# Convolving four channel blocks of the first token group on TensorE by diagonal tap matrices, with the first scores in two pieces and a new order table

## The chip, the cores and the metric

The kernel runs on one core of one Trainium2 chip. The metric is the time of one execution on the device in microseconds (us), the median over runs. The core has a matrix engine (TensorE, PE in the views; its weight loads are shown apart as PEld), a vector engine (VectorE, DVE), an activation engine (ScalarE, ACT), GpSimd (POOL) and a queue that issues DMAs (SyncE, SP). Each engine works through its own list of instructions in order; semaphores make one engine wait for another.

## What is computed

Attention with a local window and a few global keys, then a feed-forward block with a convolution along the tokens, then a gated block that mixes along the tokens. Cut to what matters here:

```
attn = softmax(scale * q @ k.T - slope * dist, on kept keys) @ v     # (2, 8, 768, 64)
x    = attn, heads joined                                            # (2, 768, 512)
h    = relu(x @ w_in)                                                # 1024 channels
conv = sum over j of conv_w[j] * h shifted by j - 1 along the tokens # 3 taps, per channel
y    = (h * sigmoid(conv)) @ w_out
u, v = halves of relu(y @ w2_in); v normalised over channels
out  = (u * (w_spatial @ v + b)) @ w2_out
```

Here `conv` is the part that moves to another engine.

## The kernel before

The tokens go in six groups of 256 (two batches of three). Group g passes through these stages.

- Attention (`tick`, `scores`, `soften`, `turn_p`, `weigh`, `turn_x`). A unit u is a pair of heads of one group, a step s one of its two tiles of 128 queries. `scores` (L789) makes the scores of both steps in float32; `soften` adds the bias and takes the lowest (L808 on VectorE), then the exponential (L826 on ScalarE); `turn_p` transposes them on TensorE (L839), `weigh` multiplies by v (L894 for the first two groups, in float32), and `turn_x` transposes the result (L942).
- First product (`inner`, L1017): 12 matmuls in float16 (parts high and low) make one block of 128 channels; there are 8 blocks in a group. Then, for that block, a relu moves it out of PSUM into the tile `hp` (L1361). The convolution follows: `middle` (L1024, on ScalarE or VectorE) writes the middle tap back into the PSUM bank, `sides` (L1030, two VectorE instructions) adds the outer two. Tanh (L1050), the gate (L1055) and the split into two float16 parts follow.
- Second product (`outer`, L1087), then the last block (`normal` L1171, `columns_u` L1382, `seventh` L1294, `last` L1444) for the whole batch.

The order of the instructions on each engine is not left to a scheduler. Python code lists the tasks with planned costs, and the table `ORDER`, a string found by a search beforehand, says which task comes next and on which engine it runs, and which PSUM bank it uses. Everything is emitted in this order, so each engine's queue is fixed by the table. Where the plan leaves TensorE idle within its first 70 us, `Plan.emit` puts in matmuls whose result nobody reads (`warm`, L988, the tile `hl`). They are called fillers below. Their count follows from the planned costs, not from what happens on the chip.

At the start, VectorE builds the masks from two counts that a small DMA brings: `word` (L567), then on TensorE `spread` (L570) copies them to all partitions, then `words` (L573) and `masks` (L578 to L585), then two biases (L594). The instructions of `flags` (L635, L637, L625) only check the counts for a branch at the end.

Of the kernel before, what the change touches and what calls it, by code (L numbers as in the profile page):

```python
# [17 lines left out]
ALU = mybir.AluOpType  # L18
# [29 lines left out]
BIASES = 2  # L48

# [58 lines left out]
def sub_cost(n):  # L108
# [6 lines left out]
    "CHSAAGAWSDnGAnSAXGABDACGAZSADDAuSAbGAgSAEDBHGCMDAFPAGDCJA0CIGAHDAaP12AJDAKAASAAIDAMAAoGAdDBaSApA3AyDAYSANGAcDAOA",  # L115
    "A2P45AzDA3SAeACKDALGAfACLDAqDA1AAwP6CNSATGAQABIDBhP12BMSBJDA0ABdDARGA-SBLABeDBKAArDEHGBFP0APGBgABbP4BfABGDAhGAxA",
    "CUP53CQDAUAAsDBcAB0DAVGBwP0AiA6BzDD9SCRDB3P4CpGDgSBxAAjDAtGCTAAkDCSAByGB1AA4GCrDCnP2A5A1BiSB4DCuP0BpSAlAA6DBTSCo",
    "AAmGCqDB2AA7DCtACOP6BOA4CvDBNGB5SDhP21CsAA_GDBDCPADADA8AC-P0BPDDDACVP3DYP6ECDC_ABQDDCADxDCWACZSBRADwDDWP5DzADZDD",
    "EP0DXAEBDDaP4DFADeP5BqGBAA1DGDCXDEEABjGBBDDbABkA6A9GDcDEFP20EDAAvSDfDDyABSGBCDBVA3DiP4FJSBlDDjAD_P1B7A5B6GDkDEAA",
    "BUGERDEPP4BmDBDADmP1EQAB8DCwSBnACASBWDEGP6DoAB9DDpABXDB-AD0P4EhDEIACgSB_GBYAESDDISDqDEJAEeSElP53ETABEGEUAEKDD2AE",  # L120
    "-P2DrAD1GEiDELADsDD3AEMDEWGCYABoGE6DBrA0E7DEfP1D4DEkAEVP6CxGEjABZGEgAFYDFXDD5AE4P3BsDEXACyA1DJGEvP5D6DEYABtDCBGE",
    "5ACzDC3SFaAEmP4E_DCCA0DtAEZDE8AFbP32DuGE9AEwGC0DFZAEnGCaGEoACDDEaAFVP1D7AC1DEpAFtDFWAC4GFsDExAF5DFqP1HbGEyAEbDCh",
    "GF6DBuAFAP6C2GCEDFrAEzDCbA3DPSFBGF9P20BvGF2SF7AEqDFvAFCAFwP1ENACcDFuAEOGE0AGIDErAGJDFDACdDGKGEcAD8GCFAFxDF3P3EdG",
    "CeAE1DCGGF4AEsDFEDCiA1GcP54E2ACfGC5A3GXDGYDHYSGMACjDFhP0FKGE3GF8AG3SC6DDKA2JzSGZGFcGGTSCkDFFADQGGLAKuSFGDEtAGGP1",
    "ClDGVAGNP6C7DGHAGWGGsDGbAGtDDRA1DLDCmGGxP3GaAG6DFjAG7DHZADSDEuGC8ADMDGuGFdP5GwAD-SF-P4C9GDTDGvAFyP2FzPDNAGODF0PF",
    "iGG4AF1PDOGGyDGCPF_AGzP1FkAG0PGADFHAG5GG_P63FlDFeAGpADHAFfDG8GGdP4GqGIQSHmDG1PGeAHnDHAP5FmAGDPGfDG9AG2PFIGGrSHOD",
# [1596 lines left out]
```

## Time and profile before

| what | value |
|---|---|
| median of 3 runs | 346.46 us (346.24 to 347.46) |
| profiled execution, its own time | 346.18 us |
| its span in the profile | 344.4 us |
| TensorE busy | 336.9 us, 98% of the span, 2824 matmul records |
| VectorE busy | 305.3 us, 89% |
| ScalarE busy | 244.0 us, 71% |
| GpSimd busy | 140.6 us, 41% |

The span runs from the first to the last instruction of the program; the execution's own time holds some 1.8 us more around it. Busy times are shares of the whole span, an average over stages with different limits. Matmul records overlap, because matmuls are pipelined: the mean duration of a record is not the time that it adds to the stream, and a busy TensorE may be working at fillers.

### The profile page before, as it was taken

To read this page: it belongs to the slowest core of one execution; us is meant where nothing else is said; L and a number is where in the kernel's file an instruction comes from. 1 tells how busy PE (TensorE), PEld (TensorE's weight loads), DVE (VectorE), ACT (ScalarE), POOL (GpSimd) and SP (SyncE) were. 2 spreads that over 40 slices of the span, in tenths; PEclk is the share of its full clock that TensorE was granted. 3 is DMA by queue.
4 is the path that set the end of the run, shared out by engine and by line. 5 is a ranking of instruction groups with operands and counts; after the bars stand their busy time and mean duration, and the time that the engine had idled before them with its cause. 6 is when DMAs were issued, how large, how long until landed. Compare 5 with 4: busy or idle time off the path is not lost.

```text
span 344.4 us, 7937 instructions
## 1 busy us (share of the span) xinstructions
PE 336.9 (98%) x2824; PEld 246.5 (72%) x2824; DVE 305.3 (89%) x892; ACT 244.0 (71%) x619; POOL 140.6 (41%) x233
## 2 busy tenths in 40 slices
PE   8999999999999999999999999999999999999993
PEld 5888779898888888888996757755556666654451
DVE  6999999999999999999988899999998999999400
ACT  4999999999999999999865552776555233334331
POOL 5747698599757877737451000000124012010000
PEclk9999999999999999999999999999999999999998
DMA  7999638799659984645770000001461000000332
GB/s 246 349 386 300 214 105 302 175 209 256 125 149 205 278 173 79 184 79 109 102 221 0 2 1 0 2 1 48 126 206 52 0 2 0 3 30 0 124 124 101
DMA packets 46115, 43.62 MB, mean 127 GB/s; under 512 B 34674, under 2 KB 36466, under 8 KB 45554
## 3 DMA queue, kind: packets, MB, share of 16 engines
q1 hardware_dynamic: 46064, 43.02, 45.7%
q8 instruction: 24, 0.39, 0.5%
q14 instruction: 25, 0.20, 0.2%
q10 hardware_dynamic: 2, 0.00, 0.0%
HBM read 31.48 MB, written 3.15 MB: 101 GB/s over the span
## 4 chain that ended last, share of the span: by engine, by line
PE 96%; DMA 1%; DVE 0%; ACT 0%; issue 0%; DVEq 0%
PE bank L1017 19%; PE bank L1087 18%; PE bank L1294 12%; PE bank L1444 9%; PE bank L1382 9%; PE bank L1171 9%; PE bank L789 7%; PE bank L894 4%; PE bank L839 2%; PE bank L988 2%; PE bank L942 2%; DMA qk_dt_float<-in_qk 1%; PE bank L900 1%; PE bank L901 1%; PE bank L902 1%; ACT wk_dt_float L454 0%
## 5 line engine op out<-in xcount | busy, mean ns | idle before, releaser
L1017 PE MATMUL bank<-x_dt_float,w1h_dt_float 128*128 128x260 f16 (+1 forms) x384 | 65.5, 273 | 0.0
L1087 PE MATMUL bank<-hh_dt_float,w2h_dt_float 128*128 128x256 f16 (+2 forms) x192 | 52.4, 273 | 0.0
L1017 PE MATMUL bank<-x_dt_float,w1l_dt_float 128*128 128x260 f16 (+1 forms) x192 | 52.4, 273 | 0.0
L1087 PE MATMUL bank<-hl_dt_float,w2h_dt_float 128*128 128x256 f16 (+2 forms) x192 | 52.3, 272 | 0.0
L1087 PE MATMUL bank<-hh_dt_float,w2l_dt_float 128*128 128x256 f16 (+2 forms) x192 | 52.3, 272 | 0.0
L1030 DVE SCALAR_TENSOR_TENSOR bank<-hp_dt_float,cwt,bank 128x254 f32<-128x254 f32 (+2 forms) x96 | 46.1, 486 | 3.3 <-ACT bank L1024 0.6
L470 POOL TENSOR_TENSOR ph_dt_float<-sb_dt_float,ph_dt_float 128x512 f16<-128x512 f32 x29 | 34.2, 1184 | 20.5 <-ACT ph_dt_float L456 12.4
L1017 PEld LDWEIGHTS <-w1h_dt_float 128*128 128x128 f16 x384 | 37.1, 97 | 5.7
L1087 PEld LDWEIGHTS <-w2h_dt_float 128*128 128x128 f16 x384 | 36.3, 98 | 5.4 <-issue 0.3
L808 DVE CUSTOM_DVE_ANT_0 sb_dt_float<-bank,bias_dt_float 128x256 f32<-128x256 f32 (+1 forms) x96 | 35.4, 402 | 1.6 <-PE bank L789 1.3
L1382 PE MATMUL bank<-ys_dt_float,w3uh_dt_float 128*128 128x384 f16 x128 | 31.2, 326 | 0.0
L826 ACT ACTIVATE sb_dt_float<-sb_dt_float,nb_dt_float 128x256 f32<-128x256 f32 (+1 forms) x64 | 29.6, 491 | 0.0
L659 POOL TENSOR_SCALAR raw_dt_float<-raw_dt_float 128x512 int32<-128x512 uint8 x28 | 19.0, 680 | 24.7 <-DMA raw_dt_float<-in_w 22.0
L1444 PE MATMUL bank<-w4h_dt_float,g_dt_float 128*128 128x512 f16 (+1 forms) x104 | 28.8, 363 | 0.0
L1171 PE MATMUL bank<-w3vh_dt_float,ys_dt_float 128*128 128x512 f16 x96 | 28.5, 379 | 0.0
L470 POOL TENSOR_TENSOR hl_dt_float<-ac_dt_float,hh_dt_float 128x254 f16<-128x254 f32 (+2 forms) x35 | 23.4, 678 | 10.7 <-DVE hh_dt_float L460 8.0
L1444 PEld LDWEIGHTS <-g_dt_float 128*128 128x128 f16 x156 | 15.2, 98 | 15.4
L1171 PEld LDWEIGHTS <-ys_dt_float 128*128 128x128 f16 x144 | 14.1, 98 | 15.3
L1294 PE MATMUL bank<-ws_dt_float,vn_dt_float 128*128 128x384 f16 x144 | 25.0, 326 | 0.0
L1050 ACT ACTIVATE bank<-bank 128x254 f32<-128x254 f32 (+2 forms) x48 | 16.9, 364 | 10.5 <-DVE bank L1030 10.2
L1024 ACT ACTIVATE bank<-hp_dt_float,cwt 128x254 f32<-128x254 f32 (+2 forms) x44 | 21.0, 477 | 0.5
L1055 DVE SCALAR_TENSOR_TENSOR ac_dt_float<-bank,hp_dt_float 128x254 f32<-128x254 f32 (+2 forms) x48 | 19.5, 418 | 2.0 <-ACT bank L1050 1.5
(198 smaller groups left out, 907.6 us busy)
## 6 DMA issues: line engine op xcount, KB each, us to landing
raw_dt_float<-in_w SPq DMA_DIRECT2D x20, 512.0 KB, 6.3
qk_dt_float<-in_qk SPq DMA_DIRECT2D x24, 336.0 KB, 4.6
v_dt_float<-in_vb SPq DMA_DIRECT2D x4, 1024.0 KB, 5.7
out_x<-wk_dt_float SPq DMA_DIRECT2D x11, 256.0 KB, 2.0
raw_dt_float<-in_wst SPq DMA_DIRECT2D x6, 384.0 KB, 3.8
raw_dt_float<-in_w3v SPq DMA_DIRECT2D x4, 512.0 KB, 5.5
raw_dt_float<-in_w3u SPq DMA_DIRECT2D x4, 512.0 KB, 4.4
v_dt_float<-in_vb SPq DMA_DIRECT2D x2, 768.0 KB, 5.1
```

The source lines that it names most:

```text
L470: self.engines[e].tensor_tensor(out=out, in0=in0, in1=in1, op=ALU.subtract)
L789: nc.tensor.matmul(self.ps(sp[h])[:, 256 * t : 256 * (t + 1)], x[r, t * P : (t + 1) * P], y[r, k0[t] : k0[t] + 256], start=n == 0, stop=n ...
L808: nc.vector.tensor_tensor_reduce(out=sb[:, h, :n], in0=self.ps(self.sp[u][h])[:, 256 * t : 256 * t + n], in1=self.m("bias", 2 * p + h)[:, ...
L826: nc.scalar.activation(out=sb[:, h, :n], in_=sb[:, h, :n], func=AF.Exp, scale=-1.0, bias=nb[:, h : h + 1])
L1017: nc.tensor.matmul(self.ps(acc)[:, :nx], w[f][:, k * P : (k + 1) * P], x[:, k, x0:], start=k == n == 0, stop=k == 3 and n == 2,)
L1024: nc.scalar.activation(out=ac(), in_=near(1), func=AF.Copy, scale=tap(1))
L1030: nc.vector.scalar_tensor_tensor(out=ac(), in0=near(j), scalar=tap(j), in1=ac(), op0=ALU.mult, op1=ALU.add)
L1087: nc.tensor.matmul(ps(), w[2 * d + k // 4][:, k % 4 * P : (k % 4 + 1) * P], x, start=k == n == 0, stop=k == 7 and n == 2,)
L1171: nc.tensor.matmul(ps(), x[:, y, k, tk], w[k], start=n == 0, stop=n == 11)
L1294: self.nc.tensor.matmul(self.ps(acc)[:, :HS], v[:, k, x, ek], w[:, k, y], start=n == 0, stop=n == 8)
L1382: nc.tensor.matmul(ps(), w[e4][:, k * P : (k + 1) * P], x[:, y, k, s], start=n == 0, stop=n == 11)
L1444: nc.tensor.matmul(ps(), x[:, y, k, tk], w[k][:, at], start=n == 0, stop=n == 11)
```

## The change

In group 0, blocks 0 to 3 are convolved on TensorE. For each, GpSimd makes three 128x128 matrices in float32 that hold one tap of each channel on the diagonal (`spread`, 12 instructions in all), and TensorE multiplies them with the three shifted views of `hp` and adds up in the PSUM bank (`convolve`, 12 matmuls of 254 columns in float32). `middle` and `sides` fall away for these four blocks: 4 instructions on ScalarE, 8 on VectorE. The scores of units 0 and 1 become two tasks each, one for each step, with the same matmuls, so that the first step's scores are released sooner. `flags` may not start before a planned 60 us, and the small load of the taps not before 3 us; the planned landing of the first DMA moves from 3.2 to 2.6 us and the planned start of `word` from 3.1 to 2.62 us. `ORDER` was searched anew, so the order of the whole program moves. Of all TensorE instructions only two kinds change in number: 12 tap matmuls come, and the fillers go from 60 to 18. Of these 18, 12 stand ahead of the first scores, 3 and 1 ahead of the first product, and 2 behind the third set of tap matmuls. The last output blocks also change places: before, the last product is 128x512; now it is one of 128x256.

```diff
-    BEGIN, FIRST, TURN = 0.75, 3.2, 2.0
+    BEGIN, FIRST, TURN = 0.75, 2.6, 2.0
...
+            over["ys1"] = ("taps",)
...
-        add(dict(DVE=0.17), word, writes=[("word", 0)], begin=3.1)
+        add(dict(DVE=0.17), word, writes=[("word", 0)], begin=2.62)
...
-            [("craw", 0)], 24576,
+            [("craw", 0)], 24576, begin=3.0,
...
-        add(dict(DVE=1.0), flags, reads=[("word", 0)], writes=[("flag", 0)], both=True)
+        add(dict(DVE=1.0), flags, reads=[("word", 0)], writes=[("flag", 0)], both=True, begin=60.0)
...
-        self.plan.add(dict(PE=cost), products, reads=reads, writes=sp, half=True)
+        if u >= SINGLE:
+            self.plan.add(dict(PE=cost), lambda e: products(range(2)), reads=reads, writes=sp, half=True)
+            return
+        for t in range(2):
+            self.plan.add(
+                dict(PE=0.5 * (cost + 0.283)), lambda e, t=t: products([t]), reads=reads,
+                writes=[(*x, t) for x in sp], half=True,
+            )
...
-        add(dict(ACT=scaled(nout), DVE=dve(nout) + 0.1), middle, reads=[("hp", n), ("cwt", 0)], writes=[acc])
-        add(dict(DVE=0.94), sides, reads=[("hp", n), ("cwt", 0)], writes=[acc])
+        if self.half and g == 0 and f < TAPPED:
+            taps = self.m("taps", f).rearrange("p (j n) -> p j n", j=3)
+
+            def spread(e):
+                for j in range(3):
+                    nc.gpsimd.tensor_scalar(
+                        out=taps[:, j], in0=self.ident, scalar1=tap(j), scalar2=None, op0=ALU.mult
+                    )
+
+            def convolve(e):
+                for j in range(3):
+                    nc.tensor.matmul(ac(), taps[:, j], near(j), start=j == 0, stop=j == 2)
+
+            add(dict(POOL=0.85), spread, reads=[("cwt", 0), ("ident", 0)], writes=[("taps", f)])
+            add(
+                dict(PE=3 * (0.01 + 4 * nout / 2400)), convolve, reads=[("hp", n), ("taps", f)], writes=[acc],
+            )
+        else:
+            add(
+                dict(ACT=scaled(nout), DVE=dve(nout) + 0.1), middle, reads=[("hp", n), ("cwt", 0)], writes=[acc],
+            )
+            add(dict(DVE=0.94), sides, reads=[("hp", n), ("cwt", 0)], writes=[acc])
```

`SINGLE` is 2 and `TAPPED` is 4. The order table moves instructions in three places that matter below.

VectorE at the start of the program, before (`cnt` and `within` are of `flags`, `wf` holds the spread counts, `bias` the first two bias tables):

```order
L561 TENSOR_SCALAR keep_dt_float_80<-rel_dt_float_79 128x288
L562 TENSOR_TENSOR keep_dt_float_80<-keep_dt_float_80,rel_dt_float_79 128x288
L567 CAST word<-wt 1x8
L635 CAST cnt<-wt 1x2
L637 SCALAR_TENSOR_TENSOR cnt<-cnt,word 1x2 x3
L625 TENSOR_SCALAR within<-cnt 1x1 x3
L573 COPY wf<-bank 128x8
L578 TENSOR_SCALAR few<-keep_dt_float_80,wf 128x32
```

The same place now:

```order
L573 CAST word<-wt 1x8
L567 TENSOR_SCALAR keep_dt_float_80<-rel_dt_float_79 128x288
L568 TENSOR_TENSOR keep_dt_float_80<-keep_dt_float_80,rel_dt_float_79 128x288
L579 COPY wf<-bank 128x8
L584 TENSOR_SCALAR few<-keep_dt_float_80,wf 128x32
```

`word` stands ahead of the two 128x288 instructions, and the seven instructions of `flags` are gone from here (they stand some 180 rows further on).

SyncE's first loads, before (`qk` holds queries and keys of a unit, `craw` the taps, `raw` a block of weights, `v` the values):

```order
L514 DMA craw<-in_cw 128x24
L514 DMA qk_dt_float_88<-in_qk 128x672
L514 DMA raw_dt_float_128<-in_w 128x512
L514 DMA qk_dt_float_122<-in_qk 128x672
L514 DMA qk_dt_float_130<-in_qk 128x672
L514 DMA raw_dt_float_126<-in_w 128x512
```

And now:

```order
L520 DMA qk_dt_float_88<-in_qk 128x672
L520 DMA qk_dt_float_122<-in_qk 128x672
L520 DMA qk_dt_float_130<-in_qk 128x672
L520 DMA craw<-in_cw 128x24
L520 DMA raw_dt_float_128<-in_w 128x512
L520 DMA v_dt_float_89<-in_vb 128x12x128
```

The first unit's load is issued first, and the first three units' loads stand ahead of the taps and of all weights.

TensorE behind the first blocks of the first product, before (the last weight load and matmul of a block, then attention work, then the next block):

```order
L1017 LDWEIGHTS w1l_dt_float_99
L1017 MATMUL bank<-x_dt_float_155,w1l_dt_float_99 128x256
L789 MATMUL bank<-qk_dt_float_88 128x256 x4
L894 MATMUL bank<-v_dt_float_89,pt_dt_float_131 128x65 x8
L839 MATMUL bank<-ident,sb_dt_float_132 128x128 x4
```

Now, behind the first block:

```order
L1030 LDWEIGHTS w1l_dt_float_100
L1030 MATMUL bank<-x_dt_float_155,w1l_dt_float_100 128x256
L852 MATMUL bank<-ident,sb_dt_float_123 128x128 x4
L907 MATMUL bank<-v_dt_float_89,pt_dt_float_131 128x65 x8
L1071 MATMUL bank<-hp_dt_float_188,taps_dt_float_189 128x254 x3
L852 MATMUL bank<-ident,sb_dt_float_132 128x128 x4
L795 MATMUL bank<-qk_dt_float_130 128x256 x4
L852 MATMUL bank<-ident,sb_dt_float_139 128x128 x4
L907 MATMUL bank<-v_dt_float_89,pt_dt_float_144 128x65 x8
```

Three tap matmuls stand behind a transpose and a `weigh`, with the relu of their block to be done meanwhile. Two blocks of the first product follow, then six tap matmuls at once; two more blocks later the last three stand directly behind the fifth block's matmuls.

## Rows read from the trace of the kernel before

**Rows 1.** The page: busy us, share of the span and instructions of each engine.

```profile
PE 336.9 (98%) x2824; PEld 246.5 (72%) x2824; DVE 305.3 (89%) x892; ACT 244.0 (71%) x619; POOL 140.6 (41%) x233
```

**Rows 2.** Stretches: length; PE, PEld, DVE, ACT, POOL busy (instructions); clock; DMA.

```profile
40.00:50.00 10.00, 9.87 (x81) 7.61 (x79) 9.82 (x31) 9.97 (x27) 8.23 (x16) 1.00 0.45 135
50.00:60.00 10.00, 9.90 (x87) 8.83 (x87) 9.69 (x31) 10.00 (x24) 8.73 (x16) 1.00 0.74 249
```

**Rows 3.** The same for the fillers (L988) alone: PE and PEld busy (records).

```profile
0.00:8.45 8.45, 4.54 (x23) 2.68 (x23) 1.00 0.71 249
8.45:70.00 61.55, 5.90 (x38) 3.47 (x37) 1.00 0.78 261
```

**Rows 4.** Chain that ended last: start us, length us, what (records).

```profile
1.19 2.10 PE bank L988 x9
...
4.07 1.44 PE bank L988 x6
5.50 2.01 PE bank L789 x8
...
8.49 1.06 PE bank L789 x8
...
13.88 1.73 PE bank L894 x16
15.61 0.44 PE bank L839 x4
...
28.19 3.94 PE bank L1017 x36
...
42.16 0.87 PE bank L988 x8
```

**Rows 5.** Timeline of the start: start us, length us, engine, line, out<-in, count [idle before <-releaser].

```profile
2.61 0.15 DVE L567 CAST word<-wt 1x8 f32<-1x8 uint16 x1
...
3.22 0.59 PE L570 MATMUL bank<-word,ones 1*128 1x8 f32 x2
...
3.85 0.17 DVE L573 COPY wf<-bank 128x8 f32<-128x8 f32 x1 [0.17 <-PE bank L570]
...
5.41 1.11 ACT L603 ACTIVATE bias_dt_float<-rel_dt_float 128x288 f32<-128x288 f32 x3 [2.48 <-DVE rel_dt_float L585]
5.42 0.83 DVE L594 SCALAR_TENSOR_TENSOR bias_dt_float<-rel_dt_float,keep_dt_float 128x288 f32<-128x288 f32 x2
...
7.56 0.33 DVE L808 CUSTOM_DVE_ANT_0 sb_dt_float<-bank,bias_dt_float 128x160 f32<-128x160 f32 x1 [1.31 <-PE bank L789]
...
9.49 0.66 PE L839 MATMUL bank<-ident,sb_dt_float 128*128 128x128 f32 x4
```

**Rows 6.** Loads of `qk` in the first 14 us: issue to landing.

```profile
DMA to landing us min/median/max: 3.2/4.9/7.6
```

**Rows 7.** Groups by line and shape, 20 to 70 us: busy us, mean ns | idle.

```profile
L826 ACT ACTIVATE sb_dt_float<-sb_dt_float,nm_dt_float 128x256 f32<-128x256 f32 x18 | 8.4, 502 | 0.0
L655 ACT ACTIVATE bank<-raw_dt_float 128x512 f32<-128x512 f32 x12 | 7.6, 637 | 0.0
...
L1024 ACT ACTIVATE bank<-hp_dt_float,cwt 128x254 f32<-128x254 f32 x8 | 3.8, 471 | 0.1
...
L1030 DVE SCALAR_TENSOR_TENSOR bank<-hp_dt_float,cwt,bank 128x254 f32<-128x254 f32 x16 | 7.6, 483 | 0.3
```

**Rows 8.** Timeline of TensorE around its two longest waits, columns as in group 5.

```profile
22.40 0.38 PE L988 MATMUL bank<-hl_dt_float 128*128 128x256 f16 x2
22.91 0.44 PE L942 MATMUL bank<-ident,xk_dt_float 128*128 128x128 f32 x2
...
48.94 0.93 PE L988 MATMUL bank<-hl_dt_float 128*128 128x256 f16 x7
50.10 1.14 PE L789 MATMUL bank<-qk_dt_float 64*128 64x256 f32 x8 [0.23 <-DMA qk_dt_float<-in_qk]
```

**Rows 9.** The end: timeline of ScalarE's last copies out of PSUM.

```profile
333.62 0.38 ACT L454 ACTIVATE wk_dt_float<-bank 128x256 f32<-128x256 f32 x1 [2.27 <-PE bank L1444]
...
338.75 0.60 ACT L454 ACTIVATE wk_dt_float<-bank 128x512 f32<-128x512 f32 x1 [1.67 <-PE bank L1444]
```

More of the change, by code (lines that the diff above doesn't have):

```diff
@@ L48 @@
 BIASES = 2
+SINGLE = 2
+TAPPED = 4
 HALF = dict(w=8, x=9, h=12, y=12, g=12, v=8, s=16)
@@ new lines @@
+    "AfAA4PA0DAgABASANGBKDASAAxP4CPSCLA0A2AARGBjP56AhSBLDA1ABfDBMABgDATGBNAAyDBHP2AqA1CKGDpGBdP3ApGCMDB1DBIAB2DB0GCND",
+    "BiAArDAVGB5P4BeAAsDELGB4ABhACSDBrSB3AA6GCTDByP2A7A0DiSB6DCQP3BOSCVACWP15A8DBVSBBGCUACRAD3GD5GA9DBzACpP4CtDBCA6B7",
+    "SCXP3CrGCsDDjP02DDDCuADCDAiGCvABDDCqADAP1DEADzDCwP4DyDDFABEDAjA5EDDD1ACCSEEDBFAD_SDYP6AkDDBAEHP02CxDBPGDZAEGABsG",
+    "AlDDaP1CYAD0AETDBWGBkSEFAEUDEgSCZDAtAFLSAmDEWADGP6B8GDbDEBP4BXA5DgP3AnGEjDDHABQA1BYDECAFMGEkDCDGBRDEmAERP0AwSA-A",
+    "EnP24DhDEVADIDBlGElABSDEhP3ESAAuGDkP6E9DEiADcP1CbSFaDE6P0DlAE8DFdP34A_GDdADmDCaADeDE7AFZDEaGE_AEIP1BZDGVSE-AF4SF",
@@ new lines @@
+    "vDBmA6FuDCiSFXP2BTDFxABnDFAP5BUGEKAFwAF7DFbABoDB9A0BaDCySFcAEMPF8DBbGBpAFBDFYAB-DFsP6DrGF-AF_P45BtA3B_DCcGDJABuD",
+    "DKSENABGGF5P2FtAGKDFyP0EODF9AGaDBqGDfAGZDEPABvDCAAEQGDoP6GLDCdA4C5SF6DEyGCzGCkA3CeDC0A5CBGD2P1FzDDqABwACfDDLGDsP",
+    "CEA2C1DGMGD4ACjGCgACFDBxGD6PDtAC2DDMA0DuDGbGGOAClDC6GGeP45GNACGDChGD7AGcACmDGIP6GXAHaSGPP2DNDDRSDvAGYGCnAD8DGJAG",
+    "vDGuDDwGGdAFfP3G8DCHAGzP6EYGG9DFeGFgAGwGGQDEpGCIGC7A1FhDC3AC8DGAP4G-GGyAEASC4GGfP5DODEXP2GxAG6AC9DG_AG0DG7GHBP30",
+    "HAAGrAEZDHMDGBAEoP1ISSHbAHpDGsGHoDG5SGgAGCDD9AGhDEbPHcGGtSEqAHPDErAHQDDnAEsDHCP6EcAFCP4D-GFRAEdDHRGHDAFSDEtAExP5",
@@ new lines @@
+    "HTAFDGFEDHNGEeAEuDFFAHEDFNAFGDIKP3FkGEfGHOSEzAFTAFODEvAFjP0E0AFUDHSAE1DEwGFHAFPAF0P2DSGF1PDTA1FIDF2PFQDFlAF3PE2A",
+    "HtP64HmACODDxAFmAGEPE3DHnGJLSITADUDICP5GWSFJAH8DHqGILACoGIYDHsAFnDGGP4E4AGHPHrAE5GGRPDVDFoAGSPC-AIUGGTPFpDGFPDPA",
+    "H7DHUP1IDDIMAIXDFqAIAP0FKDH4AH9GINDFrGGUPH-AGjPDWAIZGIgP6IBDH5GIEAIaAHVDIbAH6SIzGGnPDQGIOAIFDGkPIhAIcP01GlAH_AIP",
+    "DDXGIiDIGAGoPIVAHWP7I1DI0DHXPIwAIjDIWGIdP3HYPHiAHZPJMAIHDHyPI2GIxDHzPIIAH0PIkAJSDJNGH1PIySIeAGmDHvP5HgAI7P1IlDJR",
+    "DH2AI3AIfDI4AJTDHjDJWP26JPAHhDKESJUAG1P0I8AH3DJQGJVAG2PJvDJuDG3PFVAI9DI5P3JwGKKDC_GKJDIoP7IQAI6DGpAJqAKLGHuGI-DJ",
@@ L170 @@
+    "P4cfDcYDdSDdKP7clDcoDc4DdjP6b5DczDdXDdsP2a3Dc0DcsDamDdkDdlDdvP5dTDdtAc5DbiAduScFDanDbjAcGGavDctP6dwAa8Da9DbkAb_D",
+    "dmDb6Ac1P3dnDcBAcrDcuDcHAdpP2c-DcNAdLDcTAdMDcaAcADc_DcgAdEP5dADdqAcZDcmAdrSdBDdxSddP4dCDc6Dc8Ac7DdFDd4P6c2DdeDdY",
+    "DdZDd1P7dfDdUDdaDdbDdGDdHDdyP1dgDd2AdNDdODdIDdhDd9P2dzAd5AdDAd6SdJAdPAeDP3dVAdcAd-AdiAd_SeAP0d0SdoAd3Sd7P4eGP5d8",
+    "DeBAeCSeMP7eHAeEAeFSeJP1eNAeOSePP6eKAeLSeISeQAeRS",
 )
@@ L366, in __init__ @@
         m.place(0, ("g0", 3072, 1), ("g1", 3072, 1))
+        m.place(m.at["ys1"][0], ("taps", 3 * P, 8))
         end = m.place(uv, ("u0", 3072, 1), ("vn0", 3072, 1))
@@ L509, in decide, with load @@
         self.plan.add(dict(DVE=6.0), judge, reads=[acc, ("flag", 0)], writes=[("junk", 0)])
-    def load(self, out, in_, writes, size, reads=()):
+    def load(self, out, in_, writes, size, reads=(), begin=0.0):
         self.plan.add(
             dict(SP=Plan.ISSUE), lambda e: self.nc.sync.dma_start(out=out, in_=in_), reads=reads, writes=writes,
-            load=0.05 + size / Plan.RATE,
+            load=0.05 + size / Plan.RATE, begin=begin,
         )
@@ L782, in scores, with products @@
         sp = self.sp[u] = [self.plan.next("ps") for _ in range(2)]
-        def products(e):
-            for t in range(2):
+        def products(ts):
+            for t in ts:
                 for n, (x, y) in enumerate(pairs):
@@ L812, in soften @@
             add(
-                dict(DVE=0.08 + 0.00105 * n), lowest, reads=[self.sp[u][h], ("bias", 2 * p + h)],
+                dict(DVE=0.08 + 0.00105 * n), lowest, reads=[(*self.sp[u][h], t), ("bias", 2 * p + h)],
                 writes=[("sb", s, h), ("nm", s, h)],
```

91 lines of the change are left out of this document (36 added, 55 removed).

## Prediction

> **What bounds the kernel now.** First the page's busy times [rows 1]: TensorE is busy for 98% of the span, VectorE for 89%, ScalarE for 71%. This is an average, so next the stretches [rows 2]: between 40 and 60 us VectorE and ScalarE are as full as TensorE (9.7 to 10.0 of every 10 us). Here busy shares don't tell which of the three sets the pace. The fillers do help: 23 of them start in the first 8.45 us and 37 behind that, the last of them before 54 us [rows 3]; they are work that nobody waits for. Then the chain that ended last [rows 4]: from 1.19 us on it is TensorE's own stream, fillers among it, nearly step by step. Its lengths are the prices used below, since they are what a group adds to the stream: 36 float16 matmuls of 256 columns take 3.94 us, 0.109 each; 8 fillers take 0.87 us, 0.109 each; a unit's scores 1.06 us; a unit's `weigh` (8 matmuls, 16 records) 1.73 us; 4 transposes 0.44 us. The stream has two waits that one can see [rows 8]: two fillers that start at 22.40 need 0.22 us, and the next matmul starts at 22.91, 0.29 us late; seven fillers from 48.94 need 0.76 us, and the scores behind them start at 50.10, 0.40 us late. So from 8.5 us to the end TensorE's stream is the bound, in which every item costs its price: useful work, 37 fillers and some 0.7 us of waits. What happens ahead of 8.5 us sets when this stream gets going. The sum is therefore a ledger of TensorE.
>
> **The change part by part**, against the profiled execution's 346.18 us.
>
> *Fillers.* Of the 37 behind the start, 6 are left: 31 x 0.109 = -3.4 us. That is a gain only if the useful work behind each can start at once; what it would wait for is counted under new waits.
>
> *Tap matmuls.* Twelve float32 matmuls of 254 columns over full 128 rows; the trace has none. Bounds: a unit's scores are four float32 matmuls of 256 columns over 64 rows in 1.06 us, so 0.265 each if each has the array to itself, 0.53 each if two row halves run side by side [rows 4]. That gives 3.2 to 6.4 us for twelve. Between them decide rows of full height: four float32 transposes of 128 columns take 0.44 us, one record each, 0.11; a filler of 256 float16 columns takes the same. So a record of float32 streams half as many columns in the same time, and a true float32 matmul leaves two records (`weigh`: 16 records for 8 matmuls). Four times the float16 price: 4 x 0.109 x 254/256 = 0.43 each, +5.2 us for twelve. I take 5.2.
>
> *What falls away on the other engines.* 8 VectorE instructions of 0.48 and 4 on ScalarE of 0.47 [rows 7]: 3.9 and 1.9 us. Neither engine is on the chain, so this costs and gives nothing itself; it is cover against new waits. GpSimd's 12 instructions lie on an engine that is 41% busy; they need only the taps (`craw`), long before the relus. `flags` moves behind 50 us on VectorE, some 1 us of work; on TensorE nothing waits for it.
>
> *The start.* Now: `word` is made at 2.61, ahead of `spread` at 3.22, which stands behind nine fillers (2.10/9 = 0.23 each) [rows 4, 5]. With seven, `spread` starts 0.4 us sooner, at 2.8; `word` is then also there, for it no longer stands behind two 128x288 instructions. The copy to `wf` follows 0.63 later (3.22 to 3.85), at 3.45, and from it to the end of the two biases it takes 2.40 us (3.85 to 6.25): 5.85 us. Before, VectorE then idled for 1.31 us until the scores were done, and took the first lowest at 7.56. Five fillers (0.24 each) from 3.7 on end at 4.9. The first unit's load, first in SyncE's queue, is issued 0.45 us sooner and landed 3.2 us after its issue at the quickest [rows 6], so it is there. The scores run at the lower clock level (2.01 us for a unit at 5.50, 1.06 at 8.49; the records show the step from 1.2 to 2.4 GHz between them): the first piece ends at 5.9, when the biases do. The lowest starts 1.65 us sooner. ScalarE has five biases of 0.37 to make first (from 5.0 to 6.9), then two exponentials: 7.6. TensorE meanwhile ends unit 0 at 6.9 and unit 1 between 7.9 and 8.9; with the clock's step where it is now, near 7.4, at 8.2. So the first transpose, now at 9.49 with the same two units done, starts at 8.2: -1.3 us (from -0.6 to -1.9).
>
> *Waits that go.* Both waits of [rows 8] stand behind fillers and at places that are ordered differently now: -0.6 us, between nothing and -0.7.
>
> *New waits.* With its fillers gone TensorE comes sooner to what others must make. At the first tap group the relu has 0.44 + 1.73 us of cover (a transpose and a `weigh`), at the others one block, 12 x 0.109 = 1.3 us. I take one wait like the longer one seen, +0.4 us; bounds nothing and 2.5 (second rival).
>
> *The end.* The last copy out of PSUM is now one of 256 columns instead of 512, 0.38 for 0.60 us [rows 9]: -0.2 us. The rest of the stream behind 60 us has the same matmuls in another order and cost.
>
> Sum: 346.18 - 3.4 + 5.2 - 1.3 - 0.6 + 0.4 - 0.2 = 346.3 us. The median of the runs shown is 0.28 above the profiled execution and they spread over 1.2 us, so I leave it at 346.3. In short: TensorE takes on some 5.2 us of taps, gives up 3.4 us of fillers and gets going 1.3 us sooner, and this nearly cancels. A measurement of this kernel tells 0.5%, 1.7 us, from no change.
>
> **The rivals.**
>
> *Cheaper taps, and no new waits.* If a float32 matmul has its lower bound, 0.265 us, twelve cost 3.2 instead of 5.2, and without the new wait the time is 346.3 - 2.0 - 0.4 = 343.9. For it: a unit's four matmuls do take 1.06. Against it: these read only 64 rows each, and the rows of full height say 0.43. Without the cheaper taps, the start at its best (-1.9) and no new wait give 345.3, still within the bound. Chance 0.18 for this side, with whatever else the new order may save.
>
> *ScalarE sets the pace (slower).* In the new order 22 ScalarE instructions stand from the first tapped block's relu to the relu of the third: five exponentials (8.4/18 = 0.47 each), six L655 (7.6/12 = 0.63), eleven others of some 0.45 (the mean of both is 0.55; copies and casts are a bit less): about 11 us [rows 7]. TensorE has between those places 1.3 of taps, 0.44 + 1.06 + 0.44 + 1.73 of attention and two blocks, 2.6: 7.6 us, before the six tap matmuls. If ScalarE reaches the first relu no sooner than TensorE's block ends, the second tap group waits 11 - 7.6 - 1.3 = 2.1 us, and the third some more: 346.3 - 0.4 + 2.5 = 348.4. It decides from the point where ScalarE's lead at the first taps is under 2 us. For it: ScalarE is full between 40 and 60 us. Against it: it starts its exponentials sooner, and is relieved of 1.9 us. Chance 0.12.
>
> *The clock rises later (slower).* In the rows 23 fillers come before the clock's step; now 12 do, and the work behind them is scores and transposes. If the step comes only after the third unit's scores and the first three transposes, unit 1 ends at 8.9 (0.7 later), the third unit takes 0.95 more, and 12 transposes 0.11 more each, 1.3: 346.3 + 2.9 = 349.2. Against it: from 8.5 to 22.4 us before there was no filler at all, only scores, transposes and `weigh`, and the stream kept its faster prices [rows 4]. Chance 0.05. The Trainium skill has a rule on this side (TensorE: Matmul & The Clock Gate, "Part 4: PE-mode transpose"): transposes don't count as activity for the clock as matmuls do. By that rule the new start, with fewer fillers and more transposes, risks the lower level, and the time would be the one just given; the trace shows transposes among matmuls at the faster price, and doesn't show the new mix.
>
> **How the numbers follow.** The ledger's own case (345 to 347.5) has 0.65, the faster side 0.18, the two slower ones 0.12 and 0.05. Faster by over 0.5% (under 344.7): 0.19; within: 0.64; slower (over 348.2): 0.17. The predicted time is the ledger's, 346.3. The range cuts off about one in ten on each side: down to 344.2, between the faster rival and the ledger's best; up to 348.4, the ScalarE rival.
>
> **What would show it.** In the profile after: 24 records of tap matmuls adding some 1.3 us for each three; 18 fillers; first transpose near 8.2 us with the clock's step near 7.4; VectorE's first lowest near 5.9; no wait of TensorE over 0.5 us between 9 and 70 us; the last output copy 0.38 us. The prediction is wrong if three taps take clearly less or more than 1.3 us, if TensorE stands idle at the second or third tap group, if the first transpose is not sooner than 9 us, or if TensorE's stream behind 60 us opens gaps that it did not have.

## The result, and the profile after

| kernel | median | runs | ratio, 95% interval |
|---|---|---|---|
| before | 346.67 us | 346.24 to 347.46 | |
| changed | 350.25 us | 349.18 to 351.68 | 1.0094 (1.0073 to 1.0116) |

The change costs 0.9%, outside the range that was given. The profiled execution of the changed kernel took 351.57 us with a span of 349.6, so against the profiled 346.18 us of before 5.4 us have to be found. That is more than the medians differ (3.6 us): it is one of two executions of the six, 351.57 and 351.68 us, in which TensorE's mean granted clock was 0.990; the other four had 0.995 to 0.998, as the kernel before has, and took 349.18 to 350.70 us. First the page's busy times, as in [rows 1]:

```profile
PE 339.6 (97%) x2806; PEld 249.0 (71%) x2806; DVE 304.6 (87%) x887; ACT 243.5 (70%) x615; POOL 153.5 (44%) x242
```

TensorE's share falls from 98 to 97% although it has more to do: the span has grown more than its work. Next the fillers by stretches, as in [rows 3] (length; PE and PEld busy with records; clock; DMA), and then the tap matmuls alone:

```profile
0.00:8.20 8.20, 2.90 (x12) 1.54 (x12) 1.00 0.79 257
8.20:70.00 61.80, 1.16 (x6) 0.58 (x6) 0.97 0.78 262
```

```profile
28.00:70.00 42.00, 6.59 (x24) 4.77 (x24) 0.96 0.68 214
```

Both counts are as forecast, 18 fillers and 24 records of taps; at the full clock one tap record follows the other after 0.214 us, 24 x 0.214 = 5.1 us. But the clock of the stretches behind 8.2 us is 0.97 and 0.96, where it was 1.00. (The 1.00 of the first stretch isn't borne out by its records: a filler takes 0.24 us there, and 0.11 later.) The start, as in [rows 5]:

```profile
4.80 3.58 PE L795 MATMUL bank<-qk_dt_float 64*128 64x256 f32 x16
...
8.30 0.66 PE L852 MATMUL bank<-ident,sb_dt_float 128*128 128x128 f32 x4
```

```profile
6.92 0.32 DVE L821 CUSTOM_DVE_ANT_0 sb_dt_float<-bank,bias_dt_float 128x160 f32<-128x160 f32 x1 [1.11 <-PE bank L795]
```

The first transpose comes at 8.30 us instead of 9.49; 8.2 was forecast. The scores stand in one row of 16 records, and VectorE's first lowest comes 0.64 us sooner than before, not 1.65. Now TensorE's longest waits, by what ended them (total us, times, longest); the lines for fillers of the start are left out here and below:

```profile
PE bank L907 <- DVE wk_dt_float L676: 1.3, 1, 1.3
...
PE bank L913 <- DMA pt_dt_float<-ph_dt_float: 1.0, 1, 1.0
```

The timeline of TensorE around both:

```profile
31.13 0.60 PE L852 MATMUL bank<-ident,sb_dt_float 128*128 128x128 f32 x4
33.08 1.97 PE L907 MATMUL bank<-v_dt_float,pt_dt_float 128*128 128x65 f32 x16 [1.35 <-DVE wk_dt_float L676]
34.89 2.40 PE L1071 MATMUL bank<-hp_dt_float,taps_dt_float 128*128 128x254 f32 x6
...
143.24 0.27 PE L1120 MATMUL bank<-hh_dt_float,w2l_dt_float 128*128 128x258 f16 x1
144.46 0.20 PE L913 MATMUL bank<-vh_dt_float,pt_dt_float 128*128 128x65 f16 x1 [0.95 <-DMA pt_dt_float<-ph_dt_float]
```

For 33.08 the view names VectorE's `wk`, a weight tile that the `weigh` doesn't read; its inputs are `pt` and `v`. SyncE's queue, and the load's size and time from issue to landing, say what it was:

```profile
25.60 0.68 SPq L520 DMA_DIRECT2D v_dt_float<-in_vb  x1
```

```profile
v_dt_float<-in_vb SPq DMA_DIRECT2D x1, 1024.0 KB, 7.3
```

The second group's v is issued at 25.60 us, when the last `weigh` of the first group has read the tile that it overwrites, and lands 7.3 us later, at 32.9; the `weigh` starts at 33.08. The same three rows of the kernel before:

```profile
25.11 0.68 SPq L514 DMA_DIRECT2D v_dt_float<-in_vb  x1
```

```profile
v_dt_float<-in_vb SPq DMA_DIRECT2D x1, 1024.0 KB, 6.5
```

```profile
33.12 2.00 PE L894 MATMUL bank<-v_dt_float,pt_dt_float 128*128 128x65 f32 x16
```

There v landed 6.5 us after 25.11, at 31.6, and its `weigh` started at 33.12 without a wait: TensorE had three blocks of the first product and a unit's scores to do first, where now it has one block. What the wait brought with it shows in the stretches behind it (length; PE busy; clock; DMA):

```profile
31.00:33.00 2.00, 0.73 (x7) 1.00 0.96 348
33.00:35.00 2.00, 1.92 (x17) 1.00 1.04 415
35.00:36.00 1.00, 1.00 (x5) 0.67 1.04 407
36.00:37.00 1.00, 1.00 (x4) 0.50 0.85 336
37.00:38.00 1.00, 1.00 (x5) 0.50 0.13 53
38.00:39.00 1.00, 1.00 (x7) 0.62 0.67 82
39.00:41.00 2.00, 2.00 (x20) 1.00 0.55 221
```

From 35 to 39 us TensorE's clock falls to its lower level, 0.50 of 2.4 GHz; this costs 0.33 + 0.50 + 0.50 + 0.38 = 1.7 us, and six tap records take 2.40 us instead of 1.5. So 1.35 + 1.7 + 0.95 = 4.0 us of this execution's 5.4 stand at two places. The four executions with a clock of 0.995 and more can't have had the 1.7.

### The profile page after: what moved, and what is told of

Same layout as the page of the kernel before. It is cut to its first block, busy times and chain, and to the rows that moved or that the text cites. A ratio compares the mean times of both kernels' runs of the same rounds, so it can differ in the third digit from the quotient of the medians.

```text
span 349.6 us, 7920 instructions
## 1 busy us (share of the span) xinstructions
PE 339.6 (97%) x2806; PEld 249.0 (71%) x2806; DVE 304.6 (87%) x887; ACT 243.5 (70%) x615; POOL 153.5 (44%) x242
## 4 chain that ended last, share of the span: by engine, by line
PE 72%; DVE 11%; DMA 3%; ACT 3%; issue 2%; POOL 1%; DVEq 0%; ACTq 0%
PE bank L1120 15%; PE bank L1327 12%; PE bank L1030 12%; PE bank L1477 9%; PE bank L1415 9%; PE bank L1204 9%; DMA pt_dt_float<-ph_dt_float 3%; PE bank L795 2%; DVE sb_dt_float L821 2%; DVE bank L1043 2%; DVE bank L671 1%; DVE ac_dt_float L1088 1%; DVE wk_dt_float L676 1%; PE bank L913 1%; PE bank L915 1%
## 5 line engine op out<-in xcount | busy, mean ns | idle before, releaser
L1120 PE MATMUL bank<-hh_dt_float,w2h_dt_float 128*128 128x254 f16 (+2 forms) x192 | 52.4, 273 | 0.0
L1120 PE MATMUL bank<-hl_dt_float,w2h_dt_float 128*128 128x254 f16 (+2 forms) x192 | 52.3, 273 | 0.0
L1120 PE MATMUL bank<-hh_dt_float,w2l_dt_float 128*128 128x254 f16 (+2 forms) x192 | 52.3, 273 | 0.0
L1043 DVE SCALAR_TENSOR_TENSOR bank<-hp_dt_float,cwt,bank 128x256 f32<-128x256 f32 (+2 forms) x88 | 42.6, 485 | 3.3 <-ACT bank L1037 0.7
L476 POOL TENSOR_TENSOR hl_dt_float<-ac_dt_float,hh_dt_float 128x254 f16<-128x254 f32 (+2 forms) x35 | 24.9, 721 | 16.9 <-DVE hh_dt_float L466 8.6
L839 ACT ACTIVATE sb_dt_float<-sb_dt_float,nb_dt_float 128x256 f32<-128x256 f32 (+1 forms) x64 | 30.3, 496 | 0.3 <-DVE r_dt_float L919 0.3
L460 ACT ACTIVATE wk_dt_float<-bank 128x512 f32<-128x512 f32 (+1 forms) x13 | 7.1, 562 | 28.6 <-PE bank L1477 28.3
L1083 ACT ACTIVATE bank<-bank 128x254 f32<-128x254 f32 (+2 forms) x48 | 17.7, 372 | 7.8 <-DVE bank L1043 6.1
L1327 PEld LDWEIGHTS <-vn_dt_float 128*128 128x128 f16 x144 | 14.1, 98 | 9.6
```

The lines of the kernel that those rows point to most:

```text
L476: self.engines[e].tensor_tensor(out=out, in0=in0, in1=in1, op=ALU.subtract)
L839: nc.scalar.activation(out=sb[:, h, :n], in_=sb[:, h, :n], func=AF.Exp, scale=-1.0, bias=nb[:, h : h + 1])
L1043: nc.vector.scalar_tensor_tensor(out=ac(), in0=near(j), scalar=tap(j), in1=ac(), op0=ALU.mult, op1=ALU.add)
L1083: dict(ACT=0.09 + 0.00082 * nout), lambda e: nc.scalar.activation(out=ac(), in_=ac(), func=AF.Tanh, scale=0.5 * 2.0 ** -self.k["h"]),
L1120: nc.tensor.matmul(ps(), w[2 * d + k // 4][:, k % 4 * P : (k % 4 + 1) * P], x, start=k == n == 0, stop=k == 7 and n == 2,)
L1327: self.nc.tensor.matmul(self.ps(acc)[:, :HS], v[:, k, x, ek], w[:, k, y], start=n == 0, stop=n == 8)
```

## The experiments

**Theory:** the late v, the clock behind it and the late transposed load make the loss. **Rivals:** another engine paces the stretch, so that a wait taken out comes back elsewhere; or the remainder is TensorE's own work. In every kernel below the fillers are held to the number and places of the kernel that it varies. The kernel before ran beside each; its median was 347.04 to 347.27 us on these chips, so ratios are compared, not times.

**1. The `weigh` later.** The order of TensorE's instructions:

```diff
 L852 MATMUL bank<-ident,sb_dt_float_123 128x128 x4
-L907 MATMUL bank<-v_dt_float_89,pt_dt_float_131 128x65 x8
 L1071 MATMUL bank<-hp_dt_float_188,taps_dt_float_189 128x254 x3
+L907 MATMUL bank<-v_dt_float_89,pt_dt_float_131 128x65 x8
```

> The changed kernel with one task of TensorE moved: the weigh of unit 4 (the first of the second token group) stands behind the first tap convolution instead of ahead of it. Theory (late v load, and a clock fall behind the wait): v still lands near 32.95 us, but TensorE convolves meanwhile; the 1.35 us wait at 33.08 shrinks to 0.4 us or less, the granted clock of 35 to 39 us stays above 0.95, all tap records last 0.21 us; the median falls from 350.25 us by 1.2 for the wait and by some 0.8 for the clock (half of the runs had the fall of 1.65): 348.2 us, 347.4 to 349.0. Rival (another engine paces this stretch, and TensorE only waits in one place instead of another): the idle time comes back within 10 us at another instruction, 349.8 to 350.5 us.

349.42 us, 1.0061 (1.0042 to 1.0081). The wait became one of 0.25 us ahead of the taps, and the clock stayed at 1.00. In its profile TensorE's stream ran 2.0 us ahead of the changed kernel's until 105 us; there it lost 1.0, at a transpose of x that waited 0.5 us for VectorE, and the wait for the transposed load was still there (0.98 us at 143.49). So the wait is real, but half of its gain is given back, as the rival has it, though 70 us later; the interval of its median overlaps that of the changed kernel.

**2. Fillers into the wait.**

```diff
-                if start < WARM_TO:
...
+                for _ in range({5: 7, 26: 5, 121: 3, 264: 1, 514: 2, 320: 12}.get(i, 0)):
```

The numbers are tasks and the fillers ahead of each; 320 is the `weigh` of unit 4, and the others are the 18 fillers of the changed kernel.

> The changed kernel with 12 more fillers (12 x 0.109 = 1.3 us) ahead of the weigh that waits for v, nothing else. Theory (the clock falls because TensorE idles there): the weigh still starts at 33.0 to 33.3 us, the granted clock of 33 to 40 us stays above 0.95, tap records 0.21 us; span 1.65 us shorter than the changed kernel's profiled 349.6; in the times the upper group of 350.7 to 351.7 us goes, median 349.4 us. Rival (the clock falls for another reason, by the tap matmuls themselves or by the chip's own state): the fall at 35 to 39 us stays in some runs, median 350.0 to 350.5 us.

348.54 us, 1.0039 (1.0022 to 1.0056), clear of the changed kernel. It tests the clock, since v came still later in the profiled execution, 8.2 us after the same issue. TensorE's timeline, and the stretches:

```profile
31.41 1.47 PE L1001 MATMUL bank<-hl_dt_float 128*128 128x256 f16 x12
33.98 1.97 PE L907 MATMUL bank<-v_dt_float,pt_dt_float 128*128 128x65 f32 x16 [1.10 <-DMA v_dt_float<-in_vb]
35.79 1.50 PE L1071 MATMUL bank<-hp_dt_float,taps_dt_float 128*128 128x254 f32 x6
```

```profile
35.00:37.00 2.00, 2.00 (x15) 1.00 0.90 363
37.00:39.00 2.00, 2.00 (x17) 1.00 0.11 43
```

The `weigh` starts 0.9 us later than in the changed kernel, and the clock holds: the tap records are back at 1.50 us for six. Now the view names v as what was waited for. One execution would not be enough, since the clock also held in four of six of the changed kernel. Over all executions, the mean clock was 0.992 or less in 5 of 18 of the kernels that leave this wait alone (two of the changed kernel's, three of run 3's, none of run 11's), and in 1 of 73 of the eight that fill or shorten it (runs 1, 2, 4 to 6, 12 to 14). So the idle time ahead of the `weigh` is what brings the clock down here, not the taps behind it, and useless work that fills it is worth having. How much of the gain is the clock's isn't shown: in the profiled execution the stream was 0.7 us ahead of the changed kernel's from 40 to 104 us and lost 0.9 near 107 us, as in the first run; by 148 us it gained 1.4, most of it where this time the transposed load was not waited for.

**3 and 4. The second wait, missed.** Both moves were to take the `weigh` of 144.46 us, but the one that they moved stands at 164.21 us (161 in the text of run 6) and had not waited.

> The changed kernel with the weigh that waited 1.1 us at 143.24 us for its transposed exponentials moved behind the next transpose of x and the next product block (1.5 us of TensorE). Theory: that wait goes, the median falls by 1.1 from 350.25 to 349.1 us (348.6 to 349.6). Rival (TensorE waits later for what hangs on this weigh, or for VectorE): the 1.1 us come back within 20 us, 350.0 to 350.5 us.

> Both moves together, the weigh of unit 4 and the weigh near 143 us. Theory: the effects add: 350.25 - 1.2 - 0.8 - 1.1 = 347.1 us (346.3 to 347.9), and the ledger of the prediction (346.3) is met within 1 us once the waits are taken out. Rival (something else paces): 349.5 us or more.

351.28 us, 1.0104 (1.0074 to 1.0133): no gain, as a move of a task that doesn't wait should have. The fourth is then the first run again: 349.42 us, 1.0075 (1.0053 to 1.0098). They tell nothing on the second wait.

**5. v early.** The second group's v gets memory of its own (where the outputs of the second product come later), so its load need not wait for the last `weigh` of the first group; every engine's order, SyncE's too, is that of the changed kernel (GpSimd has one small instruction more, for the new memory).

```diff
-        m.place(0, ("g0", 3072, 1), ("g1", 3072, 1))
+        m.place(0, ("g0", 3072, 1), ("g1", 3072, 1)); m.place(0, ("va", 4 * NPAIR * VW, 1))
...
-            v = self.m("v").rearrange("p (n d) -> p n d", d=VW)
+            v = self.m("va" if g else "v").rearrange("p (n d) -> p n d", d=VW)
```

> The changed kernel with v of the second token group in memory of its own, so that its load no longer waits for the last weigh of the first group: it is issued at 23.0 instead of 25.6 us, behind the same raw and qk loads; the order of every other task stays. Theory (the late v makes the wait at 33 us, and the wait makes the clock fall): v lands 7.3 to 8.7 us after its issue as in the runs so far (6.4 to 8.7), so at 29.4 to 31.7 us, the weigh starts at 31.7 to 32.0, no granted clock under 0.95 behind it; about 1.3 us of wait and 0.8 of clock are gained there, of which 1.0 may be given back near 106 and 142 us as in the run with the weigh moved: 348.5 us (347.8 to 349.3) where the changed kernel has 350.25, and no run above 350. Rival (not v but the releaser that the profile names, VectorE's wk): the weigh still starts near 33 us, 350 us.

348.38 us, 1.0061 (1.0037 to 1.0085): some 1.1 us better than the changed kernel's 1.0094, but the intervals overlap, and one of its seven executions took 350.93, where none was expected above 350. The profiled one, its quickest, took 347.86 us, 3.7 less than the changed kernel's, which was one of its slowest:

```profile
31.60 1.97 PE L907 MATMUL bank<-va_dt_float,pt_dt_float 128*128 128x65 f32 x16
33.40 1.50 PE L1071 MATMUL bank<-hp_dt_float,taps_dt_float 128*128 128x254 f32 x6
34.74 0.60 PE L852 MATMUL bank<-ident,sb_dt_float 128*128 128x128 f32 x4
```

```profile
va_dt_float<-in_vb SPq DMA_DIRECT2D x1, 1024.0 KB, 8.4
```

No wait, no fall of the clock. With v moved and nothing else the `weigh` moves with it, so v was the releaser, not `wk`. But the load, issued at 23.1 us, lands at 31.5, only 1.5 us sooner, since it took 8.4 us instead of 7.3. The DMA engines were full from its issue to its landing (share 1.03 up to 27 us, 0.99 behind), in the changed kernel less so at first (0.86 up to 29 us, 0.98 behind); that this made it longer is likely, and not shown. The wait for the transposed load was not there in this execution, nor in run 2's, while the changed kernel, run 1, 3 and 4 had it (0.95 to 1.0 us): it stands in some executions only.

**6. All three moves** (`weigh` of unit 4 later, v early, and the `weigh` of 144.46 us behind five outer products).

> The changed kernel with v early as above, the weigh of unit 4 behind the first tap convolution, and the weigh that waited at 143.24 us for its transposed exponentials behind five outer products (1.65 us) that stood after it. (The third and fourth run of the first batch moved a weigh that stands near 161 us instead and left this wait in place: 1.25 us at 141.27 us in the fourth.) Theory: both waits and the clock fall are gone, 347.2 us (346.4 to 348.0), the ledger's 346.3 within 1 us. Rival (something else paces 60 to 145 us and gives a new wait for each one taken out): 348.5 us or more.

348.47 us, 1.0048 (1.0031 to 1.0066): above the expectation and at the rival's 348.5, no clear gain on the fifth, with the 0.5 us at the transpose near 106 us again and a loss of 1.0 there.

**7 and 13. Taps taken back.** In the seventh all four blocks of the sixth go back to ScalarE and VectorE, in the thirteenth the last block of the twelfth.

```diff
-TAPPED = 4
+TAPPED = 0
```

(In the thirteenth `TAPPED` is 3. `middle` then stands right behind its relu, `sides` where the convolution stood.)

> The kernel of the run before without the taps: the four middle taps are ScalarE's again (right behind their relu), the side taps VectorE's at the places of the convolutions; all else as before it. TensorE has 24 records of 0.214 us = 5.1 us less to do. Theory by the ledger (TensorE's work sets the end): 5.1 us less, in part met by new waits for VectorE, which gets 4 x 0.94 us back at places where it is busy: 343.5 us (342.2 to 345.5). Rival (VectorE and ScalarE pace 28 to 66 us, so that the taps on TensorE cost nothing there): the time of the run before, within 0.7 us.

> The run before, with the fourth block's taps taken back from TensorE: ScalarE's middle right behind its relu, VectorE's sides at the place of the convolution near 51 us. TensorE has 6 records of 0.214 us = 1.28 us less. Theory (the remainder is TensorE's own work, and VectorE has room for one block near 47 us, where it idled 1.1 us in the run with v early): 347.3 us, 346.6 to 348.0, as fast as the kernel before. Rival (VectorE is at its limit there, as when all four were taken back, which cost 6.5 us): 348.5 to 350.5 us.

Seventh: 354.98 us, 1.0222 (1.0204 to 1.0240), slower than either side expected. Its timeline and its clock tell why:

```profile
32.44 1.97 PE L907 MATMUL bank<-va_dt_float,pt_dt_float 128*128 128x65 f32 x16 [1.13 <-DMA va_dt_float<-in_vb]
42.17 0.70 PE L795 MATMUL bank<-qk_dt_float 64*128 64x256 f32 x2 [0.76 <-DVE wk_dt_float L676]
45.78 1.72 PE L795 MATMUL bank<-qk_dt_float 64*128 64x256 f32 x6 [2.92 <-DVE wk_dt_float L676]
```

```profile
44.00:46.00 2.00, 0.22 (x2) 1.00 0.00 0
46.00:48.00 2.00, 2.00 (x9) 0.54 0.00 0
48.00:50.00 2.00, 2.00 (x12) 0.50 0.69 205
50.00:54.00 4.00, 4.00 (x21) 0.50 0.95 301
54.00:58.00 4.00, 4.00 (x21) 0.50 0.20 82
58.00:60.00 2.00, 2.00 (x11) 0.54 0.00 0
```

VectorE is late by 2.92 us, and then the clock stays down from 46 to 60 us, which costs 4 x 0.46 + 10 x 0.50 = 6.8 us. That run therefore mixes VectorE with the clock. The thirteenth doesn't: 349.06 us, 1.0060 (1.0036 to 1.0084), 1 us more than the twelfth (the intervals barely overlap) although TensorE has 1.28 us less to do. Two waits for VectorE, of 0.96 and 0.99 us ahead of first-product blocks, took the place of the taps:

```profile
PE bank L1030 <- DVE x_dt_float L476: 1.9, 2, 1.0
```

At this place of the order VectorE had no room for even one block.

**8. The kernel before without the 37 later fillers.**

```diff
-                if start < WARM_TO:
...
+                for _ in range({5: 9, 26: 6, 54: 8}.get(i, 0)):
```

> The kernel before with only the 23 fillers of the start (up to the first transposes) and without the 37 behind them. By the ledger of the prediction each filler lies on the path: 37 x 0.109 = 4.0 us less, 342.6 us. Rival (the fillers stand where TensorE would wait anyway): 346.2 to 347 us, the waits of the same length in their places; and if the clock falls behind such a wait, over 347 us.

348.08 us, 1.0025 (1.0014 to 1.0037). Not 4.0 us less but 0.9 more. TensorE's waits there:

```profile
PE bank L839 <- ACT pt_dt_float L456: 1.2, 1, 1.2
...
PE bank L839 <- DVE wk_dt_float L670: 0.5, 2, 0.3
PE bank L1017 <- DVE nm_dt_float L808: 0.5, 1, 0.5
```

And TensorE's busy time from 11 to 75 us, in the kernel before and here:

```profile
11.00:75.00 64.00, 63.65 (x562) 1.00 0.81 259
```

```profile
11.00:75.00 64.00, 60.30 (x520) 1.00 0.81 257
```

Idle time grew from 0.35 to 3.70 us, by most of the 4.0 taken out: the fillers of before stood in waits for ScalarE and VectorE. Why the median is 0.9 us over, and not some 0.7 under, stays open.

**9 and 10. Taps in the order of before**, with its 60 fillers and with 23 of them. In the table of the kernel before, `middle` of blocks 0 to 3 becomes GpSimd's `spread` and `sides` TensorE's `convolve`.

```diff
+SINGLE = 0
+
+TAPPED = 4
```

> The kernel before, with its own table and all its 60 fillers, and only the taps changed: the four middle tasks become GpSimd's spreading of the diagonals (moved into idle stretches of GpSimd from 19, 29 and 37 us on), the four side tasks TensorE's convolutions, at the places in the order where VectorE had them. If TensorE's work simply adds up (the ledger's +5.2 for the taps): 346.7 + 5.1 = 351.8 us, 350.5 to 352.5. Rival (VectorE, which is relieved of 4 x 0.94 us, paces 28 to 66 us, so that the taps buy back what they cost): 347 to 348.5 us.

> The same, and without the 37 fillers behind the start: taps in place of fillers (+5.1 - 4.0 us of TensorE). The kernel before without these fillers had waits in their places and came out at 348.08 us. If those waits were for VectorE and the taps relieve it: 346.5 to 348.3 us, the waits of 0.5 to 1.5 us near 42, 49 and 51 us shrink. Rival (they were for loads or ScalarE): 348.1 + 5.1 less what stands in a wait, 350.5 to 353 us.

352.65 us, 1.0158 (1.0137 to 1.0180), and 351.63 us, 1.0137 (1.0114 to 1.0159). The ledger's price for the taps holds with the fillers in place (352.65 is 5.6 us over before). Without them it is some 3.6 us over the eighth run: some cover, no more.

**11. Only the second wait**, now the right `weigh`, behind five outer products.

> The changed kernel with the weigh that really waited at 143.24 us moved behind five outer products (1.65 us), nothing else; the v load and its wait stay. Theory: the 1.1 us wait goes, 350.25 - 1.1 = 349.2 us (348.6 to 349.8) beside a kernel before of 346.7. Rival (the wait moves on, or stands there only in some executions): 350 us and more.

348.78 us, 1.0051 (1.0034 to 1.0068). The wait for the transposed load is gone and didn't come back. In the profiled execution v landed early (a wait of 0.6 us, no fall of the clock), and in all six the clock was 0.995 or more, so part of this run's gain is luck with v.

**12 and 14. Both causes out, and then also without the six later fillers.** The moves of the fifth and the eleventh together.

> The changed kernel with both waits taken out at their cause: v of the second group early (as in the fifth run) and the weigh of 143 us behind five outer products (as in the eleventh); the weigh of unit 4 stays in its place. Theory (the loss has two parts: waits and the clock behind them, some 2.3 us, and TensorE's own sum, taps +5.1 less fillers 3.8 = +1.3): 1.3 us over the kernel before, 348.4 us beside 347.1, 347.8 to 349.0, and no run above 350. Rival (the remainder is waits, too): 347.5 us or less.

> The kernel of the first run of this batch (four taps) without the six fillers behind the start (3 ahead of the first weigh, 1 ahead of the first product block, 2 near 66 us). If they lie on the path: 6 x 0.109 = 0.65 us less. If they fill waits, as the 37 of the kernel before did: no change within 0.3 us.

348.07 us, 1.0029 (1.0017 to 1.0041), and 348.05 us, 1.0032 (1.0019 to 1.0046). The six fillers that the changed kernel kept stand in waits. Of the changed kernel's 0.94% some 0.65% were v, the clock and the transposed load; 0.3%, 1.0 us, remains. Some of that is still v, which was late in the profiled executions of both (0.90 and 0.56 us of idle time), though the clock held; the twelfth's:

```profile
32.96 1.97 PE L907 MATMUL bank<-va_dt_float,pt_dt_float 128*128 128x65 f32 x16 [0.90 <-DMA va_dt_float<-in_vb]
34.77 1.50 PE L1071 MATMUL bank<-hp_dt_float,taps_dt_float 128*128 128x254 f32 x6
```

No version beat the kernel before.

## Why the prediction was wrong

The step that failed is **new waits**: +0.4 us, with bounds of nothing and 2.5. The profiled execution had 1.35 + 0.95 us of waits and 1.7 us of lower clock behind the first, 4.0 in all, and none of it at the tap groups where the step looked for it. It asked whether ScalarE's relus would be in time, and didn't go through the loads that TensorE waits for: the `weigh` moved ahead of two product blocks and a unit's scores, which had been the cover of v's load, a place where the order was printed. In the medians the two places are worth some 2.3 us (0.65%, run 12); the clock fell in two of the six executions only. That the loss is there is shown by runs 2, 11 and 12, whose intervals lie clear of the changed kernel's; run 5 names v as the cause of the first wait by its profile. Two of the prediction's own signs of error came true: a wait of over 0.5 us between 9 and 70 us, and a new gap behind 60.

- *Taps* (+5.2): right. 24 records at 0.214 us are 5.1, and 5.6 us in the order of before (run 9). In the new order the last block's were worth their cost: back on ScalarE and VectorE it took 1 us more (run 13).
- *Fillers* (-3.4): as a price of their own, wrong. In the order of before taking them out saved nothing, and the kernel was 0.9 us slower (run 8); taking out the last six saved nothing either (run 14). The sentence that every item of TensorE's stream costs its price, 37 fillers among them, is false for a stretch in which VectorE and ScalarE are as full as TensorE, which [rows 2] showed. By the sum of the next item the term holds together with an order that has useful work ready in their place.
- *The start* (-1.3) and *waits that go* (-0.6): the first transpose was 1.2 us sooner, near the forecast by luck. The clock's step was forecast near 7.4 us; in the trace the scores' records still follow each other at 0.43 us, the price of the lower level, until 7.95. But the two units took 1.87 and 1.64 us, nearly all at that level, where 2.01 had been put in for one. The split of the scores released nothing sooner: the first piece ended at 6.0 us, and the first lowest started at 6.92, right behind the second piece (6.88), whose count it waits for in the program as built. And little of the 1.9 us reached the end. In the fifth run, whose profile has neither the long wait nor the clock's fall, the last matmul ends at 339.97 us, in the kernel before at 338.71: +1.3. Taps less later fillers are 5.1 - 3.4 = +1.7, so 0.4 us is left of both terms.

```profile
338.33 0.38 PE L1444 MATMUL bank<-w4l_dt_float,g_dt_float 128*128 128x512 f16 x1
```

```profile
339.70 0.27 PE L1477 MATMUL bank<-w4l_dt_float,g_dt_float 128*128 128x256 f16 x1
```

A lead at the start is not passed on in the new order. In run 1's execution the clock rose sooner (its second unit's scores took 1.0 us); its first transposes came 0.23 us ahead of the changed kernel's 8.30, and at 16 us it was level (15.94 in the changed kernel), held, by the view, by ScalarE and then VectorE:

```profile
8.07 0.67 PE L852 MATMUL bank<-ident,sb_dt_float 128*128 128x128 f32 x4 [0.37 <-ACT sb_dt_float L839]
...
15.97 1.13 PE L795 MATMUL bank<-qk_dt_float 64*128 64x256 f32 x8 [0.16 <-DVE wk_dt_float L676]
```

Where the rest was lost stays open: no run takes the new start, or the new order behind 60 us, back alone.

- *The end* (-0.2): the last copy is one of 256 columns, 0.38 us for the 0.60 of [rows 9], as forecast, but the gain didn't reach the end: from the start of that copy to the end of the span it was 5.6 us before (338.75 to 344.4), 5.8 in the changed kernel and 5.6 in the fifth run.

```profile
343.79 0.38 ACT L460 ACTIVATE wk_dt_float<-bank 128x256 f32<-128x256 f32 x1 [0.76 <-PE bank L1477]
```

- *Rivals*: ScalarE at the second tap group didn't show, and cheaper taps fell with the 0.214 us. The clock rival had the right engine at the wrong place: at the start the clock rose some 0.5 us later than in the profile of before, but ahead of the first transposes, and it fell at 35 us behind an idle stretch. The Trainium skill describes that case (TensorE: Matmul & The Clock Gate, "HAM oscillation — how this bites in real kernels"): a wait for a load leaves TensorE's clock low for the work behind it. The rows above agree, 0.50 behind 1.35 us of idle time, and the remedy of run 2, work without use, held it at 1.00. The waits on that page are of 3 to 5 us; in the profiled execution a shorter one did it.

Without its term for new waits the ledger gave 345.9 us, 0.3 under before; the twelfth run, with most of the known causes out, is 1.0 over. These 1.3 us lie within the 2.1 that the start, the waits that go and the end were to bring, and hold some of v's wait too.

## What to carry to other kernels

When an order changes, list for each moved instruction the loads that it waits for, with their latest issue (the last reader of the tile that they overwrite) and the work that stood as cover ahead of it. Fillers in a stretch where three engines are full mark waits, and are not work that a change can save. And a wait of TensorE is to be priced with the clock that may fall behind it, which here, in two executions of six, was dearer (1.7 us) than the wait (1.35).

## What the runs showed of the hardware that was not expected

- **Idle time and the clock.** It fell to 0.50 behind idle times of 1.35 us (changed kernel, 1.7 us lost) and 2.92 us (run 7, 6.8 us lost). Behind 0.90 (run 12), 0.95 (changed, at 144.46 us), 0.99 (run 13), 1.10 (run 2, with 12 fillers ahead), 1.13 (run 7) and 1.24 us (run 8) it stayed at 1.00. These are single executions with different work around the gap; no run tells what the limit hangs on.
- **The clock's rise at the start comes at different times in executions of the same instructions.** The first 13 fillers and the first unit's scores are the same in the kernel before and in run 8. In the one the eight fillers that follow take 1.05 us, 0.11 each behind the first, and the first transposes come at 9.49 us; in the other they take 1.89, 0.23 each, and the transposes come at 10.82. So run 8's profiled execution was 1.3 us late ahead of the first filler that was taken out.

```profile
7.44 1.05 PE L988 MATMUL bank<-hl_dt_float 128*128 128x256 f16 x8
```

```profile
7.66 1.89 PE L988 MATMUL bank<-hl_dt_float 128*128 128x256 f16 x8
```

- **A load's landing is not its issue plus a constant.** The same v load, issued at 25.6 us in each, landed after 6.4 us in run 1, 7.3 in the changed kernel and 8.2 in run 2; issued at 23.1 us it took 8.4 (run 5), at 23.5 us 9.3 (run 12). The DMA engines are near full all this time (0.98 from 29 us to the landing in the changed kernel, run 1 and run 2, 0.99 from 27 us in run 5).
- **The profile's releaser** for the wait at 33.08 us, `wk` of VectorE, was wrong; that of the same wait in run 2 was right.
